# Attention and feed-forward in one program: x of block 5 transposed by DMA, and the loads and q,k transposes of blocks 6 to 8 in another order

## The chip, the cores and the metric

The kernel runs on one core of one Trainium2 chip. The metric is the device time of one execution in microseconds (us), the median over runs of the same program. A profiled execution gives, beside its own time, a span from the first to the last instruction of the program, a page of summaries, and a trace that can be asked for single instructions.

The core's engines, as the profile names them: PE (matrix products; PEld is its weight load), DVE (vector), ACT (scalar), POOL (GpSimd) and SP (which here does nothing but issue transfers). Sixteen DMA engines move data.

## The reference

Inputs are q, k and v, each (8, 8, 576, 64) in float32, and the weights w_in (512 x 2048) and w_out (2048 x 512). Attention is within chunks of 64 rows; its result, laid out as 4608 rows of 512, goes through a feed-forward layer with a squared relu.

```python
scores = scale * np.matmul(q_c, k_c.transpose(0, 1, 2, 4, 3))   # 64 x 64 per chunk and head
scores = scores - np.max(scores, axis=-1, keepdims=True)
attn = np.exp(scores)
attn = attn / (np.sum(attn, axis=-1, keepdims=True) + 1e-09)
out = np.matmul(attn, v_c)
...
h = np.maximum(x @ w_in, 0.0)
return (h * h @ w_out).astype(np.float32)
```

## The kernel before

**Groups and blocks.** The 4608 rows are cut into 18 groups of 256, and two groups make a block: block j holds groups 2j and 2j + 1. Groups 0 to 13, 16 and 17 are "whole", 256 rows of one batch. Groups 14 and 15 (block 7) are made of single chunks of four batches each, so that their loads come in twice as many and smaller pieces.

**Stages of one group's attention.** Its q and k are loaded as float32 into a staging tile `qk_st` (L266, L279), V into `ve_sb` and `vo_sb` (L308, L312). From block 2 on, q and k are cast to bfloat16 into `qkb` (`CQ` and `CK`, together `C`, L446 to L454) and transposed by one DMA of 128 x 2048 elements, `TD` (L456, issued at L460). `SC` (L464) makes the scores on PE and their exponential on ACT. `AV0` and `AV1` (L496) multiply with V for the group's two tiles of 128 rows; DVE divides (L442, L443) and leaves `x`. `XT` (L530) transposes x into `xT`: on PE through `ps_att` (L540) with a copy by ACT (L545), or, for blocks in `X_BY_DMA`, with one DMA of 128 x 1024 elements issued by SP (L535). The staging tile and the tiles of V are shared in rotation: a load into one waits until its earlier user is done.

**The feed-forward.** Blocks 0 to 3 do it in a plainer way. Blocks 4 to 8 use a scheme with seven products in place of eight for both layers. In the first layer a block is four quads, and each quad has the steps A1, B2, A6, C5, C3, A7 and A4 (`quad_step`, L678; products at L657). They read sums of xT that DVE makes once for each block, `x_sums` (L622, adds at L614): e1 from the first (even) group's xT, e2 = e1 plus the odd group's xT, then e3 and e4. A1 reads e1, A6 reads e2. Squares follow on ACT, DVE or POOL (L674, L676). The second layer of block j - 1 (`ffn_out`, L728; products at L780) is interleaved with the first of block j.

**The order of work.** It is written out by hand. From block 4 on, the function `run` (L1159) goes through ticks, one quad each, of four slots, so that a block has 16 slots; quad 0 of a block is its slots 0 to 3. At each slot it issues the quad steps, then what is planned at the slot minus one half, then a half product of the second layer, then what is planned at the slot. `at(j, s, f, g)` plans f for group g at slot s of block j's stage; s may pass 16. In the stage of block j the attention of block j + 1 is made (SC, AV0, AV1 and XT at slots S0, V0, V1 and X0, L1126), and its x sums at slots 13.5 to 18 (L1138); the loads, casts and q,k transposes of block j + 2 are planned there too (L1144 to L1155). The tile framework derives the waits; each engine, and each queue of transfers, works its own list in this order.

**SP's list.** All loads, the q,k transposes and the x transposes by DMA are issued by SP in the order of the plan; the output stores are mostly issued by POOL (L804, L809). An x transpose in SP's list waits for x, a q,k transpose for the casts, a load for its tile to be free, and what stands behind waits too. `pieces` (L927) lists the loads of a block: q and k of both groups, then V of both groups. Block 6 has 15 pieces, block 7 has 32, block 8 has 15.

Casts for block 4 are made by ACT, and by POOL later (L948), where they stand in one list with squares and stores.

The plan lines that the change touches, as they were:

```python
S0, V0, V1, X0 = ((1.5, 3.5), (4.5, 7.5), (6, 10), (8.5, 12)) if j == QUADS else (
...
if j == n_blk - 3:
    for s, n in ((0, 1), (1, 1), (2, 1), (8.5, 3), (13, 5), (15, 2), (15.5, 2)):
        at(j, s, load, n, more)
else:
    for s in range(0, 16):
        at(j, s, load, 1 if is_whole(blocks[j + 2][0]) else 2, more)
for i in range(2):
    at(j, (9, 10 if j == QUADS else 13)[i], C, blocks[j + 2][i])
    at(j, ((9.5, 14.5) if j == n_blk - 3 else (12, 13.5))[i], TD, blocks[j + 2][i])
```

`QUADS` is 4 and `n_blk` is 9, so `n_blk - 3` is block 6.

Of the kernel before, what the change touches and what calls it, by code (L numbers as in the profile page):

```python
# [144 lines left out]
def kernel(  # L145
# [22 lines left out]
    blocks = [[g, g + 1] for g in range(0, n_grp, 2)]  # L168
    n_blk = len(blocks)
# [7 lines left out]
    def is_whole(g):  # L177
        return chunks[g][0][0] == chunks[g][3][0]
# [1 line left out]


    FIRST_DMA_T = 4
    X_BY_DMA = (6, 7, 8)
    QUADS = 4
    LEAD = 4

# [60 lines left out]
    def runs(g):  # L247

        for t in range(2):
            (b, s), (b1, s1) = chunks[g][2 * t:2 * t + 2]  # L250
            if b == b1:
                yield t, 0, 2 * CH, b, s
            else:
                yield t, 0, CH, b, s
                yield t, CH, CH, b1, s1

    def loaded(g, which):
        return qk_st[g % (5 if g < 8 else 2)][:, which * 1024:which * 1024 + 1024]
# [3 lines left out]
    def qk_pieces(g):  # L262


        def pairs(which, src, p, m, b, s):
            return lambda: nc.sync.dma_start(  # L266
                out=loaded(g, which)[p:p + m // 2, :].rearrange("p (h e) -> p h e", h=H),
                in_=src[b, :, s:s + m, :].rearrange("h (s i) d -> s h (i d)", i=2))

        if is_whole(g):  # L270
            yield pairs(0, q, 0, GT, *chunks[g][0])
        else:
            for c in range(4):
                yield pairs(0, q, c * CH // 2, CH, *chunks[g][c])
        if g < FIRST_DMA_T:
            yield pairs(1, k, 0, GT, *chunks[g][0])
            return
        for t, p, m, b, s in runs(g):
            yield lambda t=t, p=p, m=m, b=b, s=s: nc.sync.dma_start(  # L279
                out=loaded(g, 1)[p:p + m, t * 512:t * 512 + 512].rearrange(  # L280
                    "p (h d) -> p h d", h=H),
                in_=k[b, :, s:s + m, :].rearrange("h s d -> s h d"))
# [3 lines left out]
    for g in range(n_grp):  # L286
        if is_whole(g):
# [3 lines left out]
            b, s = chunks[g][0]  # L291
# [12 lines left out]
    def v_pieces(g):  # L304

        even, odd = [], []
        for t, p, m, b, s in runs(g):
            even.append(lambda t=t, p=p, m=m, b=b, s=s: nc.sync.dma_start(  # L308
                out=v_even[g % NV][p:p + m, t, :, 0:D],
                in_=v[b, 0::2, s:s + m, :].rearrange("h s d -> s h d")))  # L310
        for n, p, m, b, s in odd_loads[g]:
            odd.append(lambda n=n, p=p, m=m, b=b, s=s: nc.sync.dma_start(  # L312
                out=v_odd[n % NO][p:p + m, :, 0:D],
                in_=v[b, 1::2, s:s + m, :].rearrange("h s d -> s h d")))
        if g < 2:
            yield from [even[0], *odd[:-1], even[1], odd[-1]]
        else:
            yield from even + odd
# [34 lines left out]
    def x_tile(j):  # L353
        if j not in xTs:
            xTs[j] = att_pool.tile([128, BT // 128, n_dt, 128], BF16, name="xT", bufs=2)
        return xTs[j]
# [173 lines left out]
    def transpose_x(g):  # L530
        x = state.pop(("x", g))
        n = 2 * half_of(g)
        dst = x_tile(g // 2)[:, n:n + 2].rearrange("p t h q -> p (t h) q")
        if g // 2 in X_BY_DMA:
            nc.sync.dma_start_transpose(out=dst, in_=x.rearrange("p t h a d -> p (t h a d)"))  # L535
# [15 lines left out]
    for j in range(n_blk):  # L551
        if j < QUADS:
            at = {(th, fh, h): 4 * th + 2 * fh + h
                  for th in range(2) for fh in range(2) for h in range(2)}
        else:
# [6 lines left out]
            at = {(*key, 0): s for key, s in zip(keys, old)}  # L562
# [83 lines left out]
    def tock():  # L646
        state["clock"] += 1
        for x in [x for x in later if x[0] <= state["clock"]]:
            later.remove(x)
            x[1]()  # L650
# [276 lines left out]
    def pieces(grps):  # L927
        for g in grps:
            yield from qk_pieces(g)
        for g in grps:  # L930
            yield from v_pieces(g)

    SC, AV, XT = scores, values, transpose_x
    TD = transpose_qk_dma
# [69 lines left out]
    for j in range(QUADS):  # L1004
# [3 lines left out]
        def at(slot, f, *x):  # L1008
            plan.setdefault(slot, []).append((f, x))
# [87 lines left out]
    for j in range(QUADS, n_blk):  # L1097
        if j == QUADS:
            n = 14 - LEAD
            slots = [1 + 19 * i // n for i in range(n)]  # L1100
            assert len(slots) == n
        else:
            slots = [s for s in range(4, 20) if s % 16 not in NO_OUT]
            start = 3
        if j == QUADS:
            g = blocks[QUADS + 1][1]
            between = {0: [(CK, (g, nc.scalar.copy)), (TD, (g,))]}
            for n in (0, 1, 2, 3):
                between.setdefault(n, []).append((load, (1, loads)))
            for n in (2, 2, 2, 3):  # L1110
                between.setdefault(n, []).append((x_sums, (QUADS, len([1 for z in between.values() for y in z if y[0] is x_sums]))))
            for f, x in between.get(0, []):
                f(*x)
            for i in range(LEAD):
                next(out_j)
                tock()
                for f, x in between.get(i + 1, []):
                    f(*x)
        else:
            outs[j - 1] = ffn_out(j - 1)  # L1120
            at(j, start, lambda j=j: next(outs[j - 1])())
        for s in slots:
            plan.setdefault(("out", 16 * (j - QUADS) + s), []).append(outs[j - 1])

        if j + 1 < n_blk:
            S0, V0, V1, X0 = ((1.5, 3.5), (4.5, 7.5), (6, 10), (8.5, 12)) if j == QUADS else (  # L1126
                (1.5, 7), (3.5, 8), (5, 9.5), (5.5, 10)) if j == QUADS + 1 else (
                (0.5, 7), (2, 8), (3.5, 9.5), (3.5, 10)) if is_whole(blocks[j + 1][0]) else (
                (3.5, 9.5), (5, 11), (7, 12), (8, 13))
            for i, g in enumerate(blocks[j + 1]):  # L1130
                at(j, S0[i], SC, g)
                at(j, V0[i], AV0, g)
                at(j, V1[i], AV1, g)
                at(j, X0[i], XT, g)
            if j + 2 == n_blk:
                at(j, 22, check_sums)
                at(j, 25.5, count_bad)
            for i, s in enumerate((13.5, 16 if j == n_blk - 3 else 15, 17.5, 18)):  # L1138
                at(j, s, x_sums, j + 1, i)
        if j == QUADS:  # L1140
            for s in range(4):
                at(j, 4 * s + 2, w_sums_in_place, s)
            assert next(loads, None) is None
        if j + 2 < n_blk:  # L1144
            more = pieces(blocks[j + 2])
            if j == n_blk - 3:

                for s, n in ((0, 1), (1, 1), (2, 1), (8.5, 3), (13, 5), (15, 2), (15.5, 2)):
                    at(j, s, load, n, more)
            else:  # L1150
                for s in range(0, 16):
                    at(j, s, load, 1 if is_whole(blocks[j + 2][0]) else 2, more)
            for i in range(2):
                at(j, (9, 10 if j == QUADS else 13)[i], C, blocks[j + 2][i])
                at(j, ((9.5, 14.5) if j == n_blk - 3 else (12, 13.5))[i], TD, blocks[j + 2][i])  # L1155
    tail = ffn_out(n_blk - 1)
    at(n_blk, 3, lambda: next(tail)())

# [63 lines left out]
```

## Time and profile before

| what | value |
|---|---|
| median of 3 runs | 278.4 us (278.07 to 279.46) |
| the profiled execution | 276.91 us |
| its span | 275.1 us |
| PE busy | 264.9 us (96%) |
| DVE busy | 199.2 us (72%) |
| ACT busy | 168.3 us (61%) |
| POOL busy | 89.6 us (33%) |
| granted clock of PE | 1.00 |
| moved by DMA | 55.60 MB, mean 202 GB/s |

Busy time is a union over an engine's instructions; matmuls are pipelined and their ends modelled, so that several overlap. Rows of the timeline and of the chain give the start and the length in us; "x8" is a run of eight instructions merged into one row. "SPq" is SP as an issuer: the length of such a row is the time for which the issue held SP, not the time of the transfer. In rows by tile or line, "idle before" is the time for which the engine had nothing to do ahead of the instruction, and the arrow names what ended it.

### The profile page before, as it was taken

The page shows a single profiled execution, that of the slowest core. Times are in us where ns is not written, and L with a number is a line of the kernel's source. Part 1 is how long each engine was busy: PE and PEld are TensorE (multiplying, and loading weights), DVE is VectorE, ACT ScalarE, POOL GpSimd, SP SyncE. Part 2 cuts the span into 40 slices and gives each one's busy share as a digit, 9 for nine tenths or more (in the row PEclk, how much of TensorE's full clock was granted, in tenths as well). Part 3 has the DMA queues.
Part 4 walks back from the last instruction along what each step waited for, and adds up shares of the span by engine and source line. Part 5 has one row for each costly group of instructions (what it writes and reads, how often), then busy time and mean ns, then how long its engine had stood idle before and what let it go on. Part 6 is the DMA issues. An engine that isn't in the chain of part 4 may idle for free.

```text
span 275.1 us, 7923 instructions
## 1 busy us (share of the span) xinstructions
PE 264.9 (96%) x3261; PEld 203.4 (74%) x3261; DVE 199.2 (72%) x365; ACT 168.3 (61%) x300; POOL 89.6 (33%) x122
## 2 busy tenths in 40 slices
PE   2999999999999999999999999999999999999995
PEld 2764445888774588447878888888888888888884
DVE  1457514999538592499989998799779877994752
ACT  1657614894458883877678765565746665756430
POOL 2048834240360012040245224551643212331600
PEclk9999999999999999999999999999999999999999
DMA  7999999999999999999999999697999530220223
GB/s 216 262 352 389 361 332 270 339 213 172 262 210 218 238 234 218 275 223 178 228 236 197 218 238 194 103 220 196 244 187 224 123 76 2 99 55 7 71 83 114
DMA packets 136056, 55.60 MB, mean 202 GB/s; under 512 B 104273, under 2 KB 131921, under 8 KB 136017
## 3 DMA queue, kind: packets, MB, share of 16 engines
q1 hardware_dynamic: 133248, 46.54, 74.0%
q0 software_dynamic: 2624, 8.39, 9.6%
q8 instruction: 26, 0.43, 0.6%
q10 hardware_dynamic: 144, 0.13, 0.1%
q14 instruction: 14, 0.11, 0.1%
HBM read 36.70 MB, written 9.44 MB: 168 GB/s over the span
## 4 chain that ended last, share of the span: by engine, by line
PE 87%; DMA 4%; SPq 3%; DVE 3%; ACT 1%; issue 1%; ACTq 0%; DVEq 0%
PE ps_ffn L657 22%; PE ps_out L780 22%; PE ps_ffn L579 17%; PE ps_ffn L780 14%; PE ps_ffn L901 5%; PE ps_att L510 3%; PE ps_att L540 2%; DMA vo_sb<-in_v_dram 2%; PE ps_att L483 2%; DMA xT<-x 2%; DVE gT L598 2%; SPq L266 1%; SPq L308 1%; SPq L312 1%; DVE x L443 1%; ACT e L494 1%
## 5 line engine op out<-in xcount | busy, mean ns | idle before, releaser
L579 PE MATMUL ps_ffn<-xT,w_in_bf 128*128 128x512 bf16 (+1 forms) x328 | 57.8, 333 | 0.0
L780 PEld LDWEIGHTS <-w_st 128*128 128x128 bf16 x512 | 48.9, 98 | 6.6 <-DVE w_st L614 0.5
L665 DVE CUSTOM_DVE_ANT_0 relu<-ps_ffn,w_st 128x512 f32<-128x512 f32 x60 | 39.3, 684 | 13.0 <-PE ps_ffn L657 11.6
L579 PEld LDWEIGHTS <-w_in_bf 128*128 128x128 bf16 x328 | 31.2, 98 | 21.6 <-POOL w_in_bf L334 0.2
L598 DVE TENSOR_TENSOR gT<-relu 128x256 bf16<-128x256 bf16 (+2 forms) x68 | 34.1, 537 | 17.8 <-ACT relu L590 17.3
L590 ACT ACTIVATE relu<-ps_ffn 128x256 bf16<-128x256 f32 (+2 forms) x82 | 39.4, 501 | 9.4 <-PE ps_ffn L579 8.6
L657 PE MATMUL ps_ffn<-qk_st,w_in_bf 128*128 128x256 bf16 x240 | 35.3, 273 | 0.1
L657 PEld LDWEIGHTS <-w_in_bf 128*128 128x128 bf16 x320 | 30.7, 98 | 4.1 <-issue 0.3
L809 POOL DMA_DIRECT2D out_dram<-o_sb x24 | 17.6, 733 | 43.6 <-DVE o_sb L614 23.3
L780 PEld LDWEIGHTS <-gT 128*128 128x128 bf16 x296 | 28.6, 98 | 3.3
L780 PE MATMUL ps_out<-w_out_bf,w_st 128*128 128x256 bf16 x240 | 30.8, 273 | 0.0
L699 ACT ACTIVATE w_st<-ps_ffn 128x512 f32<-128x512 f32 x20 | 11.9, 597 | 29.6 <-PE ps_ffn L657 29.6
L443 DVE TENSOR_TENSOR x<-ps_att,recs 128x512 bf16<-128x512 f32 x36 | 24.9, 692 | 1.2
L657 PEld LDWEIGHTS <-qk_st 128*128 128x128 bf16 x240 | 22.6, 98 | 3.2 <-DVE qk_st L614 0.3
L657 PE MATMUL ps_ffn<-xT,qk_st 128*128 128x256 bf16 x160 | 23.9, 273 | 0.0
L676 POOL TENSOR_TENSOR qk_st<-relu 128x512 bf16<-128x512 f32 x10 | 10.3, 1034 | 41.6 <-DVE relu L665 38.1
L494 ACT ACTIVATE e<-ps_att 128x1024 bf16<-128x1024 f32 x18 | 18.3, 1025 | 8.5 <-PE ps_att L483 8.5
L676 POOL TENSOR_TENSOR gT<-relu 128x512 bf16<-128x512 f32 x10 | 10.3, 1033 | 35.4 <-DVE relu L665 30.5
L449 POOL CAST qkb<-qk_st 128x1024 bf16<-128x1024 f32 x12 | 13.0, 1082 | 14.9 <-DMA qk_st<-in_q_dram 14.9
L674 ACT ACTIVATE gT<-relu 128x512 bf16<-128x512 f32 x28 | 17.7, 631 | 0.0
L780 PE MATMUL ps_ffn<-w_out_bf,w_st 128*128 128x256 bf16 x144 | 17.7, 273 | 0.0
L614 DVE TENSOR_TENSOR w_st<-gT,w_st 128x1024 bf16<-128x1024 bf16 x26 | 16.8, 682 | 0.0
(92 smaller groups left out, 428.7 us busy)
## 6 DMA issues: line engine op xcount, KB each, us to landing
qk_st<-in_q_dram SPq DMA_DIRECT2D x16, 512.0 KB, 5.6
out_dram<-o_sb POOLq DMA_DIRECT2D x28, 256.0 KB, 3.9
qk_st<-in_k_dram SPq DMA_DIRECT2D x24, 256.0 KB, 5.6
ve_sb<-in_v_dram SPq DMA_DIRECT2D x32, 128.0 KB, 3.9
w_st<-in_moe_w_in_dram SPq DMA_DIRECT2D x8, 512.0 KB, 5.9
w_st<-in_moe_w_out_dram SPq DMA_DIRECT2D x8, 512.0 KB, 5.5
vo_sb<-in_v_dram SPq DMA_DIRECT2D x24, 128.0 KB, 3.6
qk_st<-in_k_dram SPq DMA_DIRECT2D x4, 512.0 KB, 5.8
```

The lines of the kernel that those rows point to most:

```text
L443: nc.vector.tensor_tensor(out=x, in0=o[:, :, :, 0:D], in1=rec.to_broadcast([128, 2, n, D]), op=ALU.mult)
L494: nc.scalar.activation(out=e_out, in_=s_in, func=AF.Exp, scale=scale)
L579: nc.tensor.matmul(out=h[:, 0:n], lhsT=w_in_bf[:, dt, ft * 128:(ft + 1) * 128], rhs=xT[:, c // 128:(c + n) // 128, dt, :], start=(dt == 0) ...
L590: nc.scalar.activation(out=rl[:, 0:n], in_=h[:, 0:n], func=AF.Relu)
L598: nc.vector.tensor_tensor(out=dst, in0=src, in1=src, op=ALU.mult)
L614: nc.vector.tensor_tensor(out=out, in0=in0, in1=in1, op=op)
L657: nc.tensor.matmul(out=bank[:, f * GT:(f + 1) * GT], lhsT=a[:, dt, ft * 128:(ft + 1) * 128], rhs=b[:, :, dt, :], start=(first and f == 0 a ...
L665: nc.vector._custom_dve(TENSOR_ADD_SAT, out=out, in0=in0, in1=in1, s0=BIG, s1=0.0)
L674: engine.activation(out=dst, in_=r, func=AF.Square)
L676: engine.tensor_tensor(out=dst, in0=r, in1=r, op=ALU.mult)
L780: nc.tensor.matmul(out=out_ps, lhsT=lhsT, rhs=b[:, i, :], start=(first and i == 0 and (last or t == 0)), stop=(i == HF - 1), skip_group_ch ...
L809: dma.dma_start(out=out[t0:t0 + GT, col:col + HD].rearrange("(t p) d -> p t d", p=128), in_=o_sb.rearrange("p (t d) -> p t d", d=HD))
```

## The change

It has three parts.

1. `X_BY_DMA` takes block 5 as well: the x of groups 10 and 11 is transposed by SP's DMA (L535) in place of eight PE transposes and an ACT copy each. Both are planned one slot earlier, at 7.5 and 11 of block 4's stage.
2. In the stage of block 4, the six q and k pieces of block 6 stay at slots 0 to 5, one each. Its nine V pieces move from slots 6 to 14 to slots 11.5 to 14, and the q,k transposes from slots 12 and 13.5 to 10.5 and 12.5.
3. In the stages of blocks 5 and 6, the loads of blocks 7 and 8 form one list, q and k of 14, q and k of 15, V of 14, q and k of 16, V of 15, q and k of 17, V of 16, V of 17. The stage of block 5 takes 27 pieces of it (up to q and k of 16), that of block 6 takes the other 20 through the same iterator `more`. In the stage of block 5 the q,k transpose of 14 moves from slot 12 to 11.5. In that of block 6, the casts of 16 move from slot 9 to 3 and 4 and its q,k transpose from 9.5 to 5, those of 17 from 13 to 12.5 and from 14.5 to 13.5; V of 16 and 17 moves from slots 13 to 15.5, behind the x transpose of 15 (slot 13), to 8.5 and 10.5.

```diff
-    X_BY_DMA = (6, 7, 8)
+    X_BY_DMA = (5, 6, 7, 8)
...
-            S0, V0, V1, X0 = ((1.5, 3.5), (4.5, 7.5), (6, 10), (8.5, 12)) if j == QUADS else (
+            S0, V0, V1, X0 = ((1.5, 3.5), (4.5, 7.5), (6, 10), (7.5, 11)) if j == QUADS else (
...
         if j + 2 < n_blk:
-            more = pieces(blocks[j + 2])
-            if j == n_blk - 3:
-
-                for s, n in ((0, 1), (1, 1), (2, 1), (8.5, 3), (13, 5), (15, 2), (15.5, 2)):
-                    at(j, s, load, n, more)
+            g0, g1 = blocks[j + 2]
+            if j == QUADS:
+                more = pieces(blocks[j + 2])
+                for s, n in ((0, 1), (1, 1), (2, 1), (3, 1), (4, 1), (5, 1), (11.5, 3), (12, 2), (13, 2), (14, 2)):
+                    at(j, s, load, n, more)
+                steps = ((9, C, g0), (10, C, g1), (10.5, TD, g0), (12.5, TD, g1))
+            elif j == QUADS + 1:
+                n0, n1 = blocks[j + 3]
+                more = itertools.chain(qk_pieces(g0), qk_pieces(g1), v_pieces(g0), qk_pieces(n0),
+                                       v_pieces(g1), qk_pieces(n1), v_pieces(n0), v_pieces(n1))
+                for s in range(0, 12):
+                    at(j, s, load, 2, more)
+                at(j, 12, load, 3, more)
+                steps = ((9, C, g0), (13, C, g1), (11.5, TD, g0), (13.5, TD, g1))
             else:
-                for s in range(0, 16):
-                    at(j, s, load, 1 if is_whole(blocks[j + 2][0]) else 2, more)
-            for i in range(2):
-                at(j, (9, 10 if j == QUADS else 13)[i], C, blocks[j + 2][i])
-                at(j, ((9.5, 14.5) if j == n_blk - 3 else (12, 13.5))[i], TD, blocks[j + 2][i])
+                for s, n in ((0, 4), (0.5, 4), (5.5, 3), (8.5, 5), (10.5, 4)):
+                    at(j, s, load, n, more)
+                steps = ((3, CQ, g0), (4, CK, g0), (5, TD, g0), (12.5, C, g1), (13.5, TD, g1))
+            for s, f, g in steps:
+                at(j, s, f, g)
```

## The prediction

> **What bounds the kernel now.** I read the page first, then the busy time by stretches cut at the starts of blocks 4 to 8, then the chain of waits, then the queue that SP issues from.
>
> ```profile
> span 275.1 us, 7923 instructions
> ...
> DMA  7999999999999999999999999697999530220223
> ```
>
> ```profile
> 129.10:150.40 21.30, 21.30 (x311) 17.89 (x310) 19.18 (x37) 15.82 (x27) 8.91 (x9) 1.00 0.94 215
> 150.40:176.40 26.00, 26.00 (x347) 22.18 (x344) 24.07 (x43) 17.34 (x32) 10.62 (x11) 1.00 0.94 197
> 176.40:203.30 26.90, 26.90 (x355) 22.97 (x353) 23.23 (x39) 16.91 (x30) 11.92 (x12) 1.00 1.01 206
> 203.30:230.40 27.10, 26.90 (x354) 22.90 (x352) 22.17 (x40) 17.02 (x30) 6.94 (x8) 1.00 0.67 130
> ```
>
> The second fence has one row each for the stages of blocks 4 to 7: length, then the busy us of PE, PEld, DVE, ACT and POOL, the granted clock, the DMA share and GB/s. PE is busy for the whole of three stages and misses 0.20 us in the fourth, at full clock. So PE bounds the time, and only work taken off PE, or a wait put on it, counts. DMA is the other full resource (0.94 to 1.01), until about 217 us.
>
> ```profile
> 142.25 0.51 PE ps_att L540 x8
> 147.06 0.45 PE ps_att L540 x8
> ...
> 201.12 4.81 DMA xT<-x
> 206.02 0.56 DVE qk_st L614
> ```
>
> In the chain, the two L540 pieces are the x transposes of block 5 on PE. The DMA piece is the transposed x of group 15, issued at 201.12 and landed at 205.93; the DVE piece behind it is e2 of block 7. The timeline there says how late that is:
>
> ```profile
> 198.81 0.69 DVE L443 TENSOR_TENSOR x<-ps_att,recs 128x512 bf16<-128x512 f32 x1
> ...
> 205.22 0.69 DVE L614 TENSOR_TENSOR o_sb<-ps_out,kept 128x512 f32<-128x512 f32 x1
> ...
> 206.02 0.55 DVE L614 TENSOR_TENSOR qk_st<-qk_st,xT 128x512 bf16<-128x512 bf16 x1
> ...
> 206.62 0.61 PE L657 MATMUL ps_ffn<-qk_st,qk_st 128*128 128x256 bf16 x4 [0.20 <-DVE qk_st L614]
> ```
>
> DVE came free at 205.22 + 0.69 = 205.91, the transfer landed at 205.93, and PE's A6 step of block 7 waited 0.20 us for e2, more for DVE's turn than for the transfer. x itself was ready at 199.50. This is the one place in the steady part where a transfer already stands on PE's path, and the change moves the SP queue just there.
>
> **The change part by part.**
>
> *x of block 5 by DMA.* It removes 16 PE transposes: 0.51 + 0.45 = **0.96 us off PE**, all on the path. It also removes two ACT copies; ACT is busy 15.82 of 21.30 us in that stage, so that is worth nothing.
>
> ```profile
> L540 PE MATMUL ps_att<-ident,x 128*128 128x128 bf16 x24 | 1.8, 219 | 0.0
> ```
>
> By its own length one transpose takes 219 ns, but 24 of them keep PE busy for only 1.8 us, 0.075 each: they overlap, and the chain's 0.51 and 0.45 for eight are what PE gives up. [...]
>
> The edit adds two DMA transposes to SP.
>
> ```profile
> L535 SPq DMA_TRANSPOSE xT<-x x6: 1233/1555/2757, 162.7 to 223.9; - x6
> DMA to landing us min/median/max: 3.0/4.6/5.5
> ...
> L460 SPq DMA_TRANSPOSE qkT<-qkb x14: 1317/3058/4518, 61.7 to 206.3; - x14
> DMA to landing us min/median/max: 4.5/6.1/8.5
> ```
>
> Those are, for each tile, the ns that SP is held by one issue and the us to landing (least, median, most). An x transpose holds SP 1.2 to 2.8 us, a q,k transpose 1.3 to 4.5. SP issues in program order, so each delays everything behind it. The queue before:
>
> ```profile
> 139.29 2.10 SPq L279 DMA_DIRECT2D qk_st<-in_k_dram  x2
> ...
> 146.01 1.05 SPq L308 DMA_DIRECT2D ve_sb<-in_v_dram  x2
> 147.16 3.07 SPq L460 DMA_TRANSPOSE qkT<-qkb  x1
> ...
> 154.06 0.62 SPq L312 DMA_DIRECT2D vo_sb<-in_v_dram  x1
> 154.73 2.87 SPq L266 DMA_DIRECT2D qk_st<-in_q_dram  x4
> ...
> 172.84 2.58 SPq L312 DMA_DIRECT2D vo_sb<-in_v_dram  x4
> ...
> 176.84 2.42 SPq L460 DMA_TRANSPOSE qkT<-qkb  x1
> ...
> 191.32 2.76 SPq L535 DMA_TRANSPOSE xT<-x  x1
> 194.13 0.58 SPq L266 DMA_DIRECT2D qk_st<-in_q_dram  x1
> 194.75 1.49 SPq L279 DMA_DIRECT2D qk_st<-in_k_dram  x2
> 196.50 4.52 SPq L460 DMA_TRANSPOSE qkT<-qkb  x1
> 201.12 1.74 SPq L535 DMA_TRANSPOSE xT<-x  x1
> 202.91 1.37 SPq L308 DMA_DIRECT2D ve_sb<-in_v_dram  x2
> 204.33 1.83 SPq L312 DMA_DIRECT2D vo_sb<-in_v_dram  x3
> ```
>
> *Stage of block 4, new order.* Three more rows bear on it, the cast of k of group 12 on POOL, and on DVE x of group 11 and e2 of block 5:
>
> ```profile
> 143.28 1.04 POOL L454 CAST qkb<-qk_st 128x1024 bf16<-128x1024 f32 x1
> ```
>
> ```profile
> 146.00 0.69 DVE L443 TENSOR_TENSOR x<-ps_att,recs 128x512 bf16<-128x512 f32 x1
> ...
> 152.30 0.42 DVE L614 TENSOR_TENSOR qk_st<-qk_st,xT 128x512 bf16<-128x512 bf16 x1
> ```
>
> The q,k loads of block 6 stay where they are and end at 141.4. Then: x of group 10 (1.6) to 143.0; TD of group 12 waits for its cast, 144.3, and holds 2.4 (the 176.84 row, also with little in front of it) to 146.7; x of group 11, ready at 146.7 less the 0.5 saved, 1.6 to 148.3; five V loads at 0.52 to 150.9; TD of 13, 2.4, to 153.3; four V loads to 155.4. Before, the last V load ended at 154.68. So the queue enters block 7's loads **0.7 us late**. Bounds: with the least holds (1.2 and 1.3) the same sum ends 1.3 early; with 3.07 for a q,k and 2.76 for an x transpose it ends 3.2 late. I take 0.7, as the order waits less often on V buffers. x of 11 issued at 146.7 lands 3.0 to 4.6 later, 149.7 to 151.3, and e2 of block 5, the third row, comes 0.96 earlier than before, at 151.3: just in time. TD of 12 lands earlier than before, so the scores of 12 are safe.
>
> *Stage of block 5.* The first 24 loads and both x transposes keep their order. From 154.73 to 172.84 + 2.58 = 175.42 SP has no row that waits for data, so the 0.7 stays: 176.1. Then, each with its row: TD of 14, 2.4 (176.84), to 178.5; q,k of 16, three loads, 0.58 + 1.49 = 2.1, to 180.6; TD of 15 behind three such loads, 4.5 (the 196.50 row, the same neighbours), to 185.1; eight small V loads of 15 at 2.58 for four, 5.2, to 190.3; TD of 16 behind small V loads, 2.4, to 192.7; q,k of 17, 2.1, to 194.8; x of 14 behind them, 2.8 (191.32), to 197.6; nine V loads of 16 and 17, which now go **ahead** of x of 15, at (1.37 + 1.83)/5 = 0.64 each, 5.8, to 203.4. So x of group 15, ready at 198.5 with PE 0.96 earlier, is issued at **203.4 instead of 201.12**. TD of 16 no longer stands in front of it, but five V loads of 16 and four of 17 do, and the 0.7.
>
> Landing takes 3.0 to 4.6; those V loads are small and not held long, so I take 3.4: 206.8. e2 takes 0.55, PE starts 0.05 later: A6 at 207.4, against 206.62 before. PE would have been ready at 206.62 - 0.20 - 0.96 = 205.46. So it waits 1.9 us, where it waited 0.20. **Sum: -0.96 - 0.20 + 1.9 = about +0.8 us.**
>
> *What else moves.* The TD of 14 is issued at 176.1 and lands 4.5 to 6.1 later, 180.6 to 182.2; its reader is this row, 0.96 earlier in the new kernel, so at 182.1: a margin of -0.1 to 1.5.
>
> ```profile
> 183.04 0.45 PE L483 MATMUL ps_att<-qkT 64*64 64x64 bf16 x32
> ```
>
> The casts of 16 go on POOL five to six slots earlier and wait there for loads issued at 178.5 to 180.6; among and behind them stand squares and output stores.
>
> ```profile
> 184.04 1.03 POOL L676 TENSOR_TENSOR qk_st<-relu 128x512 bf16<-128x512 f32 x1 [3.21 <-DVE relu L665]
> 185.02 0.75 POOL L809 DMA_DIRECT2D out_dram<-o_sb  x1
> 190.95 1.03 POOL L676 TENSOR_TENSOR qk_st<-relu 128x512 bf16<-128x512 f32 x1 [5.18 <-DVE relu L665]
> ```
>
> A square has until the relu of the next one, a tick (6.9 us) later, so two casts of 1.0 fit; they cost something only if those loads land after about 187. After 217 us DMA is nearly idle, so nothing later is at risk. Waits of PE do not add up along the queue: a wait early makes a later one shorter, as SP runs by its own list.
>
> [...]
>
> **The rivals.**
>
> *The queue is in time* (26%). For it: the 4.52 hold that stood straight ahead of x of 15 is gone, and all holds in my list are upper ones. With 2.4 for TD of 15, 1.3 for x of 14, no initial lag and a landing of 3.0, x of 15 lands at 206.8 - 2.1 - 1.5 - 0.7 - 0.4 = 202.1, and e2 waits for nothing. Against it: nine more transfers in front. Time: -0.96 - 0.20 = -1.2 us, 277.2. It decides at a landing before 204.9.
>
> *The queue is later* (18%), the slower side: block 4's new list ends 3.2 late and not 0.7, and x of 15 needs the median 4.6 to land. That is 2.5 and 1.2 more: a landing at 210.5, net +4.5, 282.9 at worst. Half of both is 1.85 more, net +2.6, **281.0**, which I take. For it: DMA share 0.94 to 1.01 and 0.5 MB more to move ahead of block 7. Place: block 7's e2; from a landing after 207.4 it is slower by over 0.5%.
>
> *x of 11 late at block 5's own e2* (6%): TD of 12 held 4.5 and a landing of 5.5 give 154.4 where 151.3 is due; A6 of block 5 waits up to 3 us, and then the wait at block 7 shrinks: +2.0 at most, 280.4.
>
> *PE transposes cost their length, not their spacing* (2%): 16 x 0.219 = 3.5 us, and with the queue in time 278.4 - 3.5 - 0.2 = 274.7. The 1.8 us for 24 stands against it. [...]
>
> *It doesn't do what it says* (2%): the two transposes stay on PE. The condition at L534 is the list that the diff extends, so hardly.
>
> **How the numbers follow.** The profiled execution took 276.91 us (span 275.1 and 1.8 around it), the median of the runs shown is 278.4; I add the net to the median. The forecast (46%) is 278.4 + 0.8 = **279.2**, its own range -0.3 to +2.1 us, 278.1 to 280.5. What a measurement of this kernel can tell from no change is about 0.5%, 1.4 us. Faster by more: the 2% and 7 points of the first rival, if freed DMA or ACT time gives 0.2 us more than counted: 9%. Slower by more: the upper end of the forecast (13), the second rival (18), half of the third (3): 34%. Within: 57%. The range takes in the first rival and the second at +2.7: 277.0 to 281.1.
>
> **What would show it.** Right: no L540 of block 5, eight x transposes on SP; the last V load of 17 ahead of the x of 15; that issue at 203 to 204; PE idle before L657 in the stage of block 7, by DVE L614, of 1 to 3 us; the stages of blocks 4 and 5 about 0.5 us shorter each. Wrong: x of 15 issued before 201, or PE waits anywhere before 200 us, at scores of 14 or block 5's A6, or a POOL cast that DVE's relu waits for.

## The result and the profile after

| | before | after |
|---|---|---|
| median of 6 runs each, same chip | 277.99 us (277.59 to 279.46) | 287.33 us (284.35 to 289.23) |
| ratio, 95% interval | | 1.0321 (1.0289 to 1.0352): slower |
| the profiled execution, its span | 276.91, 275.1 us | 287.46, 285.7 us |

The kernel lost 9.3 us where 0.8 was forecast. The ratios here and below leave out executions that took over 1.5% longer than the fastest of their kernel, and the profiled executions of E1 and E3 further down are of that kind (285.23 us with a median of 281.14, and 289.64 with 284.46), so their rows say where PE waits and not how long as a rule. From the page of the changed kernel, the span and the granted clock by slices:

```profile
span 285.7 us, 7884 instructions
...
PEclk9999999999999999999999999999977999999999
```

The clock row was at 9 everywhere before; here two slices, around 210 to 220 us, show 7. The same stretches as in the prediction, blocks 4 to 7 of the changed kernel (length, busy us of PE, PEld, DVE, ACT, POOL, granted clock, DMA share, GB/s):

```profile
129.40:151.20 21.80, 20.71 (x295) 16.99 (x294) 20.56 (x38) 14.01 (x25) 8.64 (x9) 1.00 0.93 204
151.20:177.20 26.00, 26.00 (x347) 22.13 (x345) 23.67 (x42) 17.35 (x32) 10.71 (x12) 1.00 0.87 208
177.20:208.90 31.70, 27.26 (x354) 22.81 (x351) 22.68 (x39) 17.12 (x30) 12.27 (x12) 1.00 0.99 196
208.90:241.10 32.20, 30.04 (x352) 24.51 (x353) 22.77 (x41) 17.26 (x30) 6.94 (x8) 0.90 0.52 100
```

Block 4 is 0.5 us longer than before although it has 16 products fewer, block 5 is as it was, blocks 6 and 7 are 4.8 and 5.1 us longer. In the first three PE is busy no longer than before, or hardly (27.26 against 26.90), so what was added is idle time; in the fourth PE is also busy 3.1 us longer for the same products, at a mean clock of 0.90. The waits of PE in those stretches, from its timeline (start, length; in brackets the idle time before and what ended it):

```profile
149.45 0.60 PE L657 MATMUL ps_ffn<-qk_st,w_in_bf 128*128 128x256 bf16 x4 [0.99 <-DVE relu L665]
...
185.85 0.45 PE L483 MATMUL ps_att<-qkT 64*64 64x64 bf16 x32 [1.68 <-DMA qkT<-qkb]
...
208.93 1.03 PE L657 MATMUL ps_ffn<-qk_st,w_in_bf 128*128 128x256 bf16 x4 [2.69 <-DVE qk_st L614]
...
215.78 1.04 PE L657 MATMUL ps_ffn<-qk_st,qk_st 128*128 128x256 bf16 x4 [2.13 <-DVE qk_st L614]
```

They are, in order: a square for block 4's products, the scores of group 14, and e1 and e2 of block 7, which wait for the transposed x of groups 14 and 15. Four products at L657 took 0.60 us in the first row, at clock 1.00, and 1.03 and 1.04 in the last two, at 0.50 (the fence after the next). The chain of waits names the transfers behind the last three (issue, us to landing):

```profile
179.66 6.15 DMA qkT<-qkb
...
203.35 5.07 DMA xT<-x
...
211.61 3.60 DMA xT<-x
```

The account of the 10.6 us of span: 0.34 before block 4, where both programs are the same (jitter of single executions); 0.46 in block 4; in block 6 1.68 and 2.69 of waits, and 0.4 in which PE was busy longer or in small gaps; in block 7 2.13 less the 0.20 of before, and about 3.2 of half clock (next fence: 3.22 and 3.20 busy at 0.50, half of which is lost). What follows block 7 took 0.1 less.

The clock, by the stretches in which it changes:

```profile
205.33:208.74 3.41, 0.91 (x9) 0.57 (x6) 0.29 (x1) 0.60 (x1) 1.58 (x2) 1.00 1.19 170
208.74:212.15 3.41, 3.22 (x16) 2.29 (x17) 1.42 (x3) 1.12 (x2) 0.39 (x1) 0.50 0.91 204
212.15:215.57 3.42, 1.50 (x42) 1.10 (x40) 0.96 (x2) 1.02 (x1) 2.06 (x3) 1.00 1.08 210
215.57:218.98 3.41, 3.20 (x16) 2.25 (x16) 2.62 (x6) 1.71 (x3) 0.00 (x0) 0.50 1.17 124
218.98:222.39 3.41, 3.41 (x58) 2.67 (x57) 2.65 (x5) 2.03 (x4) 0.00 (x0) 1.00 0.52 102
```

The two stretches of 3.41 us in which PE was busy for 0.91 and 1.50 us are each followed by one at clock 0.50, the two in which it was busy for 3.22 and 3.20 by one at 1.00. So each of these two waits cost its length and then about 1.6 us more (an estimate: half of 3.22 and of 3.20). The mean clock was 0.986 to 0.988 in all six runs, which fits two such stretches in each (6.82 us at half clock in 285.7 is 0.988).

Last, SP's list (start, time for which the issue held SP):

```profile
142.59 3.46 SPq L535 DMA_TRANSPOSE xT<-x  x1
146.15 1.83 SPq L460 DMA_TRANSPOSE qkT<-qkb  x1
...
157.41 2.22 SPq L312 DMA_DIRECT2D vo_sb<-in_v_dram  x2
...
179.66 2.43 SPq L460 DMA_TRANSPOSE qkT<-qkb  x1
182.14 0.74 SPq L266 DMA_DIRECT2D qk_st<-in_q_dram  x1
182.94 3.78 SPq L279 DMA_DIRECT2D qk_st<-in_k_dram  x2
186.82 4.02 SPq L460 DMA_TRANSPOSE qkT<-qkb  x1
...
196.28 3.55 SPq L460 DMA_TRANSPOSE qkT<-qkb  x1
199.87 0.58 SPq L266 DMA_DIRECT2D qk_st<-in_q_dram  x1
200.50 2.75 SPq L279 DMA_DIRECT2D qk_st<-in_k_dram  x2
203.35 2.83 SPq L535 DMA_TRANSPOSE xT<-x  x1
...
211.61 1.29 SPq L535 DMA_TRANSPOSE xT<-x  x1
```

The order is the one that the prediction wrote down, item by item; each start is later than there. x of group 15 is issued at 211.61, not 203.4. These are times of one execution. E7 below has the same program up to block 7, and two rows of its list answer to the x of 14 and 15 above:

```profile
200.85 3.34 SPq L535 DMA_TRANSPOSE xT<-x  x1
...
209.62 1.29 SPq L535 DMA_TRANSPOSE xT<-x  x1
```

There the list is 2.0 to 2.5 us sooner and PE waits only 0.14 us at the scores of 14; the three other kernels below with the same program up to there (E5, E6, E15) wait 0.66 to 1.79 us. So some 2 us of the list's lateness, and a wait of under 2 us at the scores of 14, can come and go between executions.

### The profile page after: what moved, and what is told of

It is laid out like the page before. It is cut to its first block, busy times and chain, and to the rows that moved or that the text cites. A ratio compares the mean times of both kernels' runs of the same rounds, so it can differ in the third digit from the quotient of the medians.

```text
span 285.7 us, 7884 instructions
## 1 busy us (share of the span) xinstructions
PE 267.9 (94%) x3242; PEld 204.3 (72%) x3245; DVE 201.1 (70%) x365; ACT 167.1 (58%) x298; POOL 91.1 (32%) x122
## 4 chain that ended last, share of the span: by engine, by line
PE 81%; DMA 7%; DVE 5%; SPq 3%; ACT 2%; issue 1%; DVEq 0%; ACTq 0%
PE ps_ffn L657 20%; PE ps_out L780 20%; PE ps_ffn L579 16%; PE ps_ffn L780 13%; PE ps_ffn L901 5%; DMA xT<-x 3%; PE ps_att L510 2%; DMA qkT<-qkb 2%; DVE gT L598 2%; PE ps_att L483 2%; DMA vo_sb<-in_v_dram 2%; PE ps_att L540 1%; SPq L266 1%; SPq L308 1%; SPq L312 1%
## 5 line engine op out<-in xcount | busy, mean ns | idle before, releaser
L598 DVE TENSOR_TENSOR gT<-relu 128x256 bf16<-128x256 bf16 (+2 forms) x68 | 35.0, 554 | 17.5 <-ACT relu L590 17.2
L657 PE MATMUL ps_ffn<-qk_st,w_in_bf 128*128 128x256 bf16 x240 | 36.2, 278 | 3.8 <-DVE qk_st L614 2.7
L657 PEld LDWEIGHTS <-w_in_bf 128*128 128x128 bf16 x320 | 30.8, 99 | 9.1 <-DVE qk_st L614 3.0
L780 PE MATMUL ps_out<-w_out_bf,w_st 128*128 128x256 bf16 x240 | 31.6, 277 | 0.0
L657 PEld LDWEIGHTS <-qk_st 128*128 128x128 bf16 x240 | 23.0, 99 | 5.5 <-DVE qk_st L614 2.2
L657 PE MATMUL ps_ffn<-xT,qk_st 128*128 128x256 bf16 x160 | 24.4, 277 | 0.0
L676 POOL TENSOR_TENSOR gT<-relu 128x512 bf16<-128x512 f32 x10 | 10.3, 1033 | 42.1 <-DVE relu L665 42.1
L449 POOL CAST qkb<-qk_st 128x1024 bf16<-128x1024 f32 x12 | 13.8, 1150 | 25.0 <-DMA qk_st<-in_q_dram 22.3
L676 POOL TENSOR_TENSOR qk_st<-relu 128x512 bf16<-128x512 f32 x10 | 10.8, 1078 | 34.1 <-DVE relu L665 34.1
L614 DVE TENSOR_TENSOR w_st<-gT,w_st 128x1024 bf16<-128x1024 bf16 x26 | 18.5, 747 | 0.0
```

What stands on the lines that cost most here:

```text
L598: nc.vector.tensor_tensor(out=dst, in0=src, in1=src, op=ALU.mult)
L614: nc.vector.tensor_tensor(out=out, in0=in0, in1=in1, op=op)
L657: nc.tensor.matmul(out=bank[:, f * GT:(f + 1) * GT], lhsT=a[:, dt, ft * 128:(ft + 1) * 128], rhs=b[:, :, dt, :], start=(first and f == 0 a ...
L676: engine.tensor_tensor(out=dst, in0=r, in1=r, op=ALU.mult)
L780: nc.tensor.matmul(out=out_ps, lhsT=lhsT, rhs=b[:, i, :], start=(first and i == 0 and (last or t == 0)), stop=(i == HF - 1), skip_group_ch ...
```

## The experiments

Theories, by the letters that the expectations use. **A**: the two added x transposes in block 4's stage start the lateness. **B**: the new order by itself is at fault, most of all the one list for blocks 7 and 8. **C**: each wait is set by what stands ahead of that one transpose in SP's list. **D**: the bytes that DMA has to move by then set it, in whatever order. **E**: the half clock comes of PE's own idle time. **F** and **G** are about why the list is late: F, the issues hold SP by their own cost; G, the transfers are backed up behind full DMA engines, and the holds are that backlog. Diffs are against the changed kernel unless they say otherwise. Ratios are to the kernel before on the same chip. "14 | e1 | e2" are the waits of PE in the profiled execution at the scores of 14 and at A1 and A6 of block 7 ("-": under 0.15 us). The longest waits of E10 to E12 are elsewhere, for relus of ACT: 7.04, 3.95 and 3.88 us.

| run | median us | ratio (95%) | waits 14, e1, e2, us | half clock, us |
|---|---|---|---|---|
| E1, part 1 alone | 281.14 | 1.0087 (1.0050 to 1.0124) | 3.45, -, 0.20 | 3.41 |
| E2, part 2 alone | 280.68 | 1.0045 (1.0004 to 1.0087) | 1.14, -, 0.20 | 0 |
| E3, part 3 alone | 284.46 | 1.0186 (1.0108 to 1.0263) | -, 2.67, 4.34 | 10.24 |
| E4, parts 2 and 3 | 288.93 | 1.0355 (1.0297 to 1.0412) | -, 3.55, 2.30 | 3.41 + 3.41 |
| E8, parts 1 and 2 | 282.30 | 1.0180 (1.0138 to 1.0221) | 3.44, -, 0.20 | 3.41 |
| E5, V behind x of 15 | 284.67 | 1.0232 (1.0199 to 1.0265) | 1.79, 3.43, - | 6.83 |
| E6, x of 14 first too | 282.62 | 1.0162 (1.0119 to 1.0204) | 1.33, -, 3.21 | 3.41 |
| E7, waits filled | 285.44 | 1.0292 (1.0224 to 1.0359) | -, 0.94, 1.36 | 0 |
| E9, E8 with TD of 14 earlier | 280.64 | 1.0075 (1.0030 to 1.0120) | -, -, 0.98 | 0 |
| E10, V by ACT | 296.18 | 1.0644 (1.0581 to 1.0706) | | |
| E11, E8 with V by ACT | 292.85 | 1.0514 (1.0461 to 1.0568) | | |
| E12, before with V by ACT | 283.82 | 1.0195 (1.0112 to 1.0279) | | |
| E13, 12 stores left out | 283.26 | 1.0197 (1.0115 to 1.0278) | -, 1.89, 3.33 | 3.41 |
| E14, before without them | 277.39 | 0.9973 (0.9939 to 1.0006) | -, -, 0.20 | 0 |
| E15, x of block 7 on PE | 283.40 | 1.0183 (1.0116 to 1.0251) | 0.66, -, 0.20 | 3.41 |

**The parts by themselves (E1 to E4, E8).** E1 has only `X_BY_DMA` and the two slots of X0, E2 only the branch of block 4 (`j == QUADS`), E3 only the branches of blocks 5 and 6; E4 and E8 are pairs:

```diff
E4   -    X_BY_DMA = (5, 6, 7, 8)
     +    X_BY_DMA = (6, 7, 8)
     -  (6, 10), (7.5, 11)) if j == QUADS
     +  (6, 10), (8.5, 12)) if j == QUADS
E8   (blocks 5 and 6 as in the kernel before)
     +  for s in range(0, 16): at(j, s, load, 2, more)
     +  steps = ((9, C, g0), (13, C, g1), (12, TD, g0), (13.5, TD, g1))
     ...
     +  for s, n in ((0, 1), (1, 1), (2, 1), (8.5, 3), (13, 5), (15, 2), (15.5, 2)): at(j, s, load, n, more)
     +  steps = ((9, C, g0), (13, C, g1), (9.5, TD, g0), (14.5, TD, g1))
```

> The first part alone: x of block 5 by DMA (slots 7.5 and 11), all loads and q,k transposes as before. Theory A (SP's list runs late, and the two x transposes start it): they hold SP for 3 to 5 us in the stage of block 4, the x of group 15 is issued at 204 to 206 instead of 201.1, PE waits 2 to 4 us at e2 of block 7 and loses about 1.7 us of half clock behind that: 281 to 284 us. Theory B (the new order of loads is to blame, the x transposes are harmless): the 0.96 us of PE are gained, 277 to 278 us.

> The second part alone: the q,k transposes of block 6 ahead of its V, x of block 5 still on PE. Theory A: the list holds the same transfers, the queue enters block 7's loads within 1 us of before: 277.5 to 279 us. Theory B: V of block 6 moved behind two q,k transposes pushes the rest of the list by 2 us or more, and PE waits at e2 of block 7: 280 to 282 us.

> The third part alone: one list for blocks 7 and 8, x of block 5 on PE, block 6 in its old order. Theory A: without the late start the x of 14 is issued near 198 and the x of 15 near 205 to 206, behind the V loads of 16 and 17; PE waits 2 to 4 us there: 280 to 283 us. Theory B: this part carries nearly the whole loss, with both waits of over 2 us and half clock: 285 to 288 us. Rival of both (the list is fine by itself): 277 to 279 us.

> The changed kernel with the first part undone: x of block 5 on PE again, block 6 and the common list in the new order. Theory A: the list starts block 7's loads about 3 us earlier than in the changed kernel, the waits at the scores of 14 and at e1 of block 7 vanish or shrink under 1 us, one wait at e2 of block 7 is left: 280 to 283 us. Theory B: as the changed kernel or worse by the 0.96 us of PE: 287 to 288.5 us.

> The first two parts without the common list of blocks 7 and 8. Theory C: the q,k transpose of 12 is early again, so the wait at its scores that the first part alone showed (1.93 us) vanishes; the queue enters block 7's loads 3 to 5 us late, PE waits 1.5 to 3.5 us at the scores of 14, none over 1 us at block 7: 279.5 to 283 us. Rival (the two parts add up): 1.0087 and 1.0045 make 1.013, 282.5 us with both waits there.

No part gains, and each wait has its part. The timelines of PE of E1, E2 and E8 in turn, at the scores of 14:

```profile
189.93 0.45 PE L483 MATMUL ps_att<-qkT 64*64 64x64 bf16 x32 [3.45 <-DMA qkT<-qkb]
```

```profile
184.82 0.44 PE L483 MATMUL ps_att<-qkT 64*64 64x64 bf16 x32 [1.14 <-DMA qkT<-qkb]
```

```profile
186.92 0.52 PE L483 MATMUL ps_att<-qkT 64*64 64x64 bf16 x32 [3.44 <-DMA qkT<-qkb]
```

In E1 PE also waits 1.93 us at the scores of 12, whose q,k transpose there stands behind both new x transposes; with part 2's order (E8) that is gone. Part 1 pushes the q,k transpose of 14 past its reader; part 2 may do so too, but its 1.14 us lies within what E7 and the changed kernel differ by there. A6 of block 7 waits 0.20 us in both, as before. Part 3 has the waits at e1 and e2 and none at 14. E4, which has no x transpose of block 5, shows the same two waits at block 7:

```profile
213.67 1.03 PE L657 MATMUL ps_ffn<-qk_st,w_in_bf 128*128 128x256 bf16 x4 [3.55 <-DVE qk_st L614]
...
220.52 0.61 PE L657 MATMUL ps_ffn<-qk_st,qk_st 128*128 128x256 bf16 x4 [2.30 <-DVE qk_st L614]
```

So theory A falls as the one cause: without part 1 the loss is not smaller. B holds in so far as part 3 carries the most of any single part (1.0186). Whether the parts simply add up, the times leave open: adding the single losses gives 1.0132 for E8, 1.0231 for E4 and 1.0318 for all three, against 1.0180, 1.0355 and 1.0321. The profiled execution of E4 was already 6.2 us late at block 4's start, with a wait of 2.24 us and half clock at 117 us, ahead of all that was changed; how much of its 1.0355 has that source in the other runs is open.

**What stands ahead (E5, E6, E9, E15).** E5 puts the nine V loads of 16 and 17 behind x of 15 again. E6 also puts the q,k transpose of 16 and q and k of 17 behind x of 14. E9 is E8 with the q,k transpose of 14 two slots earlier. E15 is the changed kernel with block 7's x transposed on PE.

```diff
E5   -  for s, n in ((0, 4), (0.5, 4), (5.5, 3), (8.5, 5), (10.5, 4)):
     +  for s, n in ((0, 4), (0.5, 4), (5.5, 3), (13, 5), (14, 4)):
E6   +  for s, n in ((0, 4), (0.5, 4), (9, 3), (13, 5), (14, 4)):
     +  steps = ((3, CQ, g0), (4, CK, g0), (8.5, TD, g0), (12.5, C, g1), (13.5, TD, g1))
E9   +  steps = ((9, C, g0), (13, C, g1), (10, TD, g0), (13.5, TD, g1))   # E8: (12, TD, g0)
E15  -  X_BY_DMA = (5, 6, 7, 8)
     +  X_BY_DMA = (5, 6, 8)
```

> The changed kernel with the nine V loads of groups 16 and 17 put back behind the x transpose of 15 (slots 13 and 14). Theory C (PE's waits are set by what stands ahead of the x transposes of 14 and 15 in SP's list): x of 15 is issued 5 us earlier, the wait at e2 of block 7 (2.13 us) and the half clock behind it (1.6) vanish, those at the scores of 14 and at e1 stay: 283 to 284.5 us. Theory D (the bytes that DMA has to move by then set it, whatever their order): no change, 286.5 to 288 us.

> As the run before, and the x transpose of 14 ahead of the q,k transpose of 16 and of q and k of 17 too. Theory C: both waits at block 7 (2.69 and 2.13 us) shrink under 1 us and the clock stays at 1.00; the wait at the scores of 14 (1.68) stays: 279.5 to 281.5 us. Theory D: 286 to 288 us.

> The first two parts without the common list, and the q,k transpose of 14 at slot 10 of block 5's stage, so that four V loads fewer stand ahead of it. Theory C (what stands ahead in SP's list sets each wait): it lands 2 to 3 us earlier, the wait of 3.44 us at the scores of 14 shrinks to about 1, the half clock of 3.41 us behind it goes: 278 to 279.5 us, within 0.5% of the kernel before. Theory D (the bytes to be moved set it): 281.5 to 283 us as without the move.

> The changed kernel with x of block 7 transposed on PE, the common list as it is. Theory C (e1 and e2 of block 7 wait for x transposes that SP's list issues late): both waits and both stretches at half clock go, 8.0 us less against 0.96 of PE work more: 279.5 to 281.5 us, with the waits at the scores of 14 and in block 4's stage left. Rival (e1 and e2 are late for another reason, DVE's own work): 286 to 288.5 us.

E5, E9 and E15 removed the waits that they were aimed at, E6 one of its two, and each time another wait stayed or appeared. The times came out above theory C's ranges by 0.2 us (E5), 1.1 (E6 and E9) and 1.9 (E15), and below those of theory D or the rival. In E5 A6 of block 7 no longer waits; A1, which waited 2.69 us in the changed kernel, waits 3.43 (timeline of PE):

```profile
210.82 1.04 PE L657 MATMUL ps_ffn<-qk_st,w_in_bf 128*128 128x256 bf16 x4 [3.43 <-DVE qk_st L614]
```

In E6 A1 no longer waits, A6 does; first SP's list, then PE's timeline:

```profile
195.44 1.27 SPq L535 DMA_TRANSPOSE xT<-x  x1
196.81 5.03 SPq L460 DMA_TRANSPOSE qkT<-qkb  x1
201.90 0.58 SPq L266 DMA_DIRECT2D qk_st<-in_q_dram  x1
202.53 3.17 SPq L279 DMA_DIRECT2D qk_st<-in_k_dram  x2
205.80 2.32 SPq L535 DMA_TRANSPOSE xT<-x  x1
```

```profile
211.64 0.61 PE L657 MATMUL ps_ffn<-qk_st,qk_st 128*128 128x256 bf16 x2 [3.21 <-DVE qk_st L614]
```

x of 14 goes out at 195.44, 8 us sooner than in the changed kernel; the q,k transpose of 16 and q and k of 17, now between the two x, take 9.0 us from 196.81 to 205.80. In E9 the wait at the scores of 14 is gone and block 6 takes 26.9 us as before; two new ones of a microsecond stand behind it (timeline of PE, the scores of 16 and e2 of block 7):

```profile
207.56 0.45 PE L483 MATMUL ps_att<-qkT 64*64 64x64 bf16 x32 [0.97 <-DMA qkT<-qkb]
...
208.99 0.61 PE L657 MATMUL ps_ffn<-qk_st,qk_st 128*128 128x256 bf16 x4 [0.98 <-DVE qk_st L614]
```

In E15 both waits at block 7 and the half clock there are gone, and its stretch is what it was before, 27.2 us against 27.1 (its one half-clock stretch is at 75 us, ahead of all that was changed). Its block 6 takes 29.6 us against 26.9: 1.0 of PE work more, 0.66 of wait at the scores of 14, and 1.02 at an x transpose, for x. The stretch of block 7:

```profile
211.30:238.50 27.20, 27.00 (x355) 23.01 (x353) 22.29 (x40) 17.27 (x31) 6.94 (x8) 1.00 0.44 100
```

So theory C holds for the place: which transpose is late follows from what is put ahead of it. None of the orders tried has room for all; that no order has is not shown.

**The half clock (E7).** Ten unread products of 512 columns ahead of A1 of block 7 and eight ahead of A6, in time in which PE would wait:

```diff
+    FILL = {48: 10, 50: 8}
...
+            if s in FILL:
+                ps = att_bank()
+                for _ in range(FILL[s]):
+                    nc.tensor.matmul(out=ps[:, 0:512], lhsT=ident, rhs=w_out_bf[:, 0, :], start=True, stop=True)
```

> The changed kernel with ten products of 512 columns that nobody reads ahead of A1 of block 7 and eight ahead of its A6, about 2.2 and 1.7 us of PE work where PE waits 2.69 and 2.13. Theory E (the half clock comes of PE's own idle time): granted clock 1.00 through block 7, the two stretches of 3.41 us at half clock vanish, 283.5 to 285.5 us although PE does more. Rival (the clock falls for another reason, such as the load of the engines or of DMA): the stretches stay and the time is 287 to 289 us.

```profile
206.90:238.30 31.40, 28.75 (x359) 23.79 (x361) 22.67 (x42) 17.15 (x30) 6.95 (x8) 1.00 0.48 102
```

That is block 7's stretch of E7: the clock is 1.00, where it was 0.90. The four runs have mean clocks of 0.994 to 1.00, against 0.986 to 0.988. So with PE's waits there cut up by the products (0.94, 1.14 and 1.36 us in place of 2.69 and 2.13) the half clock did not come: theory E holds. The last section has the other traces. The time hardly followed, 1.0292 with an interval that holds the 1.0321 of the changed kernel: ahead of A6 the products had themselves to wait 1.14 us for their bank, and a wait that comes from a late list stays.

**Why the list is late (E10 to E14).** E10 issues the V loads of groups 12 to 17 from ACT (34 by the trace), E11 does so in E8, E12 in the kernel before. E13 leaves out the 12 output stores of blocks 3 to 5, 256 KB each, and E14 does so in the kernel before.

```diff
E10  +        v_queue = nc.scalar if g >= 12 else nc.sync
     -            even.append(lambda ...: nc.sync.dma_start(
     +            even.append(lambda ...: v_queue.dma_start(
     ...
E13  +            if QUADS - 1 <= j < QUADS + 2:
     +                return
```

> The changed kernel with the V loads of groups 12 to 17 issued by ACT's queue. Theory F (the time for which each issue holds SP is what makes the list late): 35 loads of about 0.6 us leave the list, the x transposes of 14 and 15 are issued 6 us and more earlier, the waits at block 7 go: 277.5 to 280 us. Theory G (the DMA engines are full and the holds only show it): the transfers land as late as before, waits of 2 us and more stay at block 7: 285 to 288 us.

> The first two parts without the common list, V of groups 12 to 17 by ACT's queue. Theory F: the q,k transpose of 14 has no V loads ahead of it on SP and lands in time, no wait at its scores: 277 to 278.5 us, as the 0.96 us of PE are kept. Theory G: it lands as late as with V on SP, wait of 2 to 3.5 us there: 281 to 283 us.

> The kernel before with V of groups 12 to 17 by ACT's queue. Theory F and G: SP's list is shorter but PE waited only 0.20 us in it: 277 to 278.5 us, the same within 0.5%. If ACT's own work is held up by its issues, 279 us and more.

> The changed kernel without the output stores of blocks 3 to 5 (their rows of the output are not written), 12 transfers of 256 KB on POOL's queue; SP's list is untouched. Theory G (the DMA engines are full, and SP's holds are their backlog): 3 MB less to move by block 7 shortens the holds, x of 15 is issued 4 us and more earlier, the waits of 1.68, 2.69 and 2.13 us shrink under 1 us and the clock stays: 278 to 281 us. Theory F (each issue costs SP a fixed time): list and waits as they were, 285.5 to 288 us.

> The control: the kernel before without the same 12 stores. PE waits only 0.20 us there, so both theories say 276.5 to 278.5 us; what it gains is taken off the gain of the run above.

E10 to E12 don't tell F from G. The loads keep ACT from its own work, and ACT has work on PE's path; ACT's timeline ("ACTq" is ACT as an issuer) and PE's in E10:

```profile
187.70 8.64 ACTq L313 DMA_DIRECT2D vo_sb<-in_v_dram  x4
```

```profile
197.53 1.01 PE L658 MATMUL ps_ffn<-qk_st,w_in_bf 128*128 128x256 bf16 x4 [7.04 <-ACT relu L714]
```

Four V loads kept ACT for 8.64 us: the issues themselves held it for 0.68, 1.65, 1.36 and 0.60 us, and ahead of the last one ACT stood 4.0 us, until another transfer had landed. The kernel before loses 2% by the same move (E12, where ACT stands ahead of V loads in the same way and PE waits 3.88 us for its relu). Issued by ACT in E10, V loads still held their issuer (0.60 us for one at 184.87, 1.94 for the three behind it, and the four above), so the hold belongs to the backlog or to the issue, and not to SP.

E13 bears on G. It issues the same list with fewer bytes in the queues (SP's list; the rows of x of 10, 14 and 15 answer to 142.59, 203.35 and 211.61 above):

```profile
140.60 2.43 SPq L535 DMA_TRANSPOSE xT<-x  x1
...
199.18 2.32 SPq L535 DMA_TRANSPOSE xT<-x  x1
...
207.57 1.70 SPq L535 DMA_TRANSPOSE xT<-x  x1
```

x of 14 and 15 go out 4 us sooner than in the changed kernel's profile, but only about 2 us sooner than in E7's, which hardly waited at the scores of 14 either; so that the wait is missing here tells nothing. Clear of the scatter is the hold of x of 10: 2.43 us, against 3.2 to 3.5 in the changed kernel, E5, E6, E7 and E15. And the ratio falls from 1.0321 to 1.0197, with intervals that just don't meet, while the control E14 gains 0.3%, with an interval that includes no change at all. So a part of the lateness is load on the DMA engines. It is a smaller part than theory G forecast (waits under 1 us, 278 to 281 us): A1 and A6 of block 7 still waited 1.89 and 3.33 us. The rest remains without those stores, and how much of it is the issues' own cost is open. No version here that writes its whole output beats the kernel before.

## Why the prediction was wrong

**Right.** PE bounds; the order of SP's list; that x of group 15 is late at block 7's e2 behind the V loads, a wait of 1.9 us forecast and 2.13 measured; and of the rivals "the queue is later" had the sign, with too small a size. That 1.9 and 2.13 agree is luck: the transfer was issued 8.2 us later than forecast, and PE came to that place nearly as late (A6 started at 215.78 and not 207.4), for reasons that the prediction did not have.

**The step that failed: the holds in SP's ledger, from block 4's stage on.** The ledger set each issue at a duration from before, and in the new order several kinds of issue held SP longer. Starts by the ledger and in the changed kernel:

| item | ledger | measured | late | grew by |
|---|---|---|---|---|
| end of block 6's V loads | 155.4 | 159.6 | 4.2 | |
| TD of 14 | 176.1 | 179.66 | 3.6 | -0.6 |
| q,k of 16 | 178.5 | 182.14 | 3.6 | 0.0 |
| TD of 15 | 180.6 | 186.82 | 6.2 | +2.6 |
| TD of 16 | 190.3 | 196.28 | 6.0 | -0.2 |
| q,k of 17 | 192.7 | 199.87 | 7.2 | +1.2 |
| x of 14 | 194.8 | 203.35 | 8.6 | +1.4 |
| x of 15 | 203.4 | 211.61 | 8.2 | -0.4 |

The first row was to enter 0.7 us late against before and entered 4.9 late (154.68 to 159.6), beyond the bound of 3.2. The list came to x of 10 1.2 us late (142.59 and not 141.4), and x of 10 held SP 3.46 and not 1.6; 1.3 us of that was taken up by the time that the ledger left for the cast of 12. Behind it the nine V loads took 6.6 and not 4.7 (149.90 to 153.10 and 156.19 to 159.63 in SP's list), and TD of 13 2.95 and not 2.4. Then q and k of 16 took 4.6 and not 2.1, q and k of 17 3.4 and not 2.1, and TD of 16 3.55 and not 2.4. The three terms that were taken from neighbours of the same kind and place (TD of 15, the small V loads, x of 14) were right within 0.5. E13 shows part of the reason: with the stores left out x of 10 held SP for 2.43 us and not 3.46, so this hold went with what the DMA engines had before them. Their share is 0.87 to 0.99 in these stages, and a price from one place in the list did not hold at another. The size is that of one execution: in E7 x of 14 and 15 were issued at 200.85 and 209.62, 6.1 and 6.2 us behind the ledger in place of 8.6 and 8.2, so most of the lateness is not scatter.

**The landing of TD of 14** was seen as a margin of -0.1 to 1.5 us and priced at nothing. It was issued 3.6 us late and took 6.15: the wait of 1.68 and, in E1 and E8, of over 3 (in E7 it cost 0.14).

**"Waits of PE do not add up along the queue."** They did: 1.68, then 2.69, then 2.13. The sentence holds for a list with a fixed lateness. This one fell further behind the ledger from item to item, from 3.6 to 8.6 us, while PE fell behind too. That x of 14 could be late at e1 was not looked at at all; only x of 15 was.

**The 0.96 us.** PE's busy time in block 4 fell by 0.59 (21.30 to 20.71), and that much wasn't gained either, since DVE is next there. It is busy 20.56 of 21.80 us. From the timelines of DVE and POOL:

```profile
144.97 1.21 DVE L676 TENSOR_TENSOR qk_st<-relu 128x512 bf16<-128x512 f32 x1
...
147.28 1.52 DVE L636 SCALAR_TENSOR_TENSOR w_in_bf<-w_in_bf 128x512 bf16<-128x512 bf16 x1
```

```profile
147.08 1.18 POOL L454 CAST qkb<-qk_st 128x1024 bf16<-128x1024 f32 x1 [1.43 <-DMA qk_st<-in_k_dram]
```

Two DVE instructions that take 0.68 elsewhere took 1.21 and 1.52, each beside a cast on POOL (another one ran from 144.60 to 145.64), and PE then waited 0.99 for a relu. No run was made for this. In the traces of the two kernels, from 125 us on, these are the only two of 48 DVE instructions from L676 and L636 that took over 0.74 us. Six others had a cast beside them too and took 0.68 to 0.74, so that the cast is the cause is not shown. In the runs without that wait (E6, E7, E13, E15) block 4 takes 20.9 or 21.0 us against 21.3: the gain is 0.3 to 0.4 us, not 0.96.

**Not priced: the half clock**, 3.2 of the 10.6 us. The trace of before has no wait of PE over 0.2 us in its steady part and no half clock there, so no row of it showed this.

## What to carry to other kernels

When a change puts more into a queue whose transfers are backed up, don't price its issues by rows from elsewhere: add up what is ahead of each consumer, let the bounds cover every term (the bound of 3.2 us here left the V loads of block 6 at 0.52 us each, and they took up to 1.55), and look at every consumer on the path, not at the latest one. In a list with as little slack as this one, an earlier place for one transpose is a later one for the next, so a repair at one point gains less than the wait that it removes (from E8 to E9 3.44 us of wait and 3.41 us of half clock went, and the ratio fell by 0.0105, 2.9 us). And in the changed kernel the waits of 2.69 and 2.13 us were each followed by 3.41 us at half clock, by estimate 1.6 us more than they lasted, so one late transfer can be dearer than its lateness.

## What the runs showed that was not expected

The half clock came in stretches of 3.41 us, and the two of a trace fit one grid: in the changed kernel they begin at 208.74 and 215.57, 6.83 us apart, and in E4 at 117.56 and 213.13, 28 times 3.413 apart. I cut all the traces of this case by that grid, wherever an execution had a half-clock stretch between 30 and 260 us. Of the 18 stretches in which PE was idle for 1.91 us or more, 17 were followed by half clock, among them 2.50 and 1.91 in the changed kernel, 2.24 and 3.01 in E4 and 2.42 in E5 (the other, in E11, was idle for 2.03). Of those with 0.5 to 1.73 us of idle time only the five that were themselves at half clock, with 1.01 to 1.44 idle, were followed by it. So in these traces it was not the length of a wait that told, but how much of it fell into one stretch. The second wait of E4, 2.30 us, was split between two (windows of E4, columns as above):

```profile
216.54:219.95 3.41, 1.68 (x44) 1.25 (x42) 0.69 (x1) 1.02 (x1) 2.41 (x3) 1.00 1.02 219
219.95:223.37 3.42, 2.85 (x39) 2.37 (x40) 3.30 (x8) 1.69 (x4) 0.00 (x0) 1.00 1.14 167
```

1.73 and 0.57 us idle, and the clock stayed at 1.00; of the 2.13 us in the changed kernel 1.91 fell into one stretch, and the next one ran at 0.50.

The hold of an issue did not go by the size of its load: in the changed kernel's list above, q loads of 512 KB held SP for 0.58 and 0.74 us, and the two k loads of 256 KB behind each for 2.75 and 3.78 together.
